# A linear-attention and SwiGLU kernel on one core: five early F blocks for six, x sums loaded earlier, query outputs stored in halves, down casts behind the SiLU

## Chip, cores and metric

One core of a Trainium2 chip runs the whole program. The metric is device time in microseconds, the median of the runs shown. The engines are TensorE (PE: matmuls, and PEld its weight loads), VectorE (DVE), ScalarE (ACT), GpSimd (POOL) and SyncE (SP, which only issues DMAs here). ACT and POOL issue some DMAs too, on queues of their own.

## What is computed

x has 2048 rows of 576 (D). With xn the row-wise layer norm of x:

```python
qkv = xn @ wqkv                                   # 32 heads of 18
phi = concat(softmax(q @ w_phi), softmax(-q @ w_phi))   # per head, for q and for k
o   = phi_q (phi_k^T v) / (phi_q (phi_k^T 1) + 1e-6)
s   = o @ wo
g   = silu((silu(xn @ w_gate) * (xn @ w_up)) @ w_down)  # F = 4608
out = x + s * g
```

All products are made from fp32r pieces: an operand is split into a high part (a cast on ACT) and a low part (a subtraction on DVE), and three products of the parts are summed.

## The kernel before, in words

**Layout.** The rows are two halves i of 1024, each of two column groups j of 512 (BT). xn is kept transposed in eight tiles X{i}{j}, `XB[i][j]` in the code (L69), 128 x 5 x 512: of D = 576, each holds two chunks of 128 rows with their low parts and a chunk of shared rows. F is 36 blocks (NF) of 128.

**Attention.** First the norm and the transposes; then, for 16 row tiles, keys and values with their softmax and the sums kv and z (L348); meanwhile GpSimd builds sums of blocks of x, stored in `sum_dram` (`sum_parts`, L316). Then the query stage (L402 to L500): for each pair of row tiles `q_tile` makes phi_q and its denominator, `numer` (L452) transposes it and multiplies by kv, and `project` (L470) multiplies by wo. `project` copies each 288-column half of its PSUM tile into the tile `so` (one buffer, 128 x 576) on ACT, and SyncE stores both halves with one DMA to `s_dram` (L483, L485).

**The feed-forward part, two forms.** A block f of F is handled either *early* or in the main stage.

- `early_tile(f, i, parts)` (L110) is the plain form: for each j, 14 matmuls of 512 columns for gate (`xw`, L82), SiLU on ACT, 14 for up, the product on DVE, and a store to `h_dram` (L121, SyncE). It needs the blocks `XB[i]`; its PSUM pool has two buffers. The first EARLY = 6 blocks go this way. They stand late in the program, so in the order that the planner writes out they fill PE's gaps in the attention stages.
- `gate_up` (L591) is the seven-product form over gate/up and the column groups (Strassen-Winograd): seven `product` calls (L566) of seven matmuls each, on sums of weights and sums of x. `gate_up_weights` (L532) loads a block's weights into `ld`, GpSimd forms the sums (L557 to L560), ACT and DVE split them (L548), and in the first pass they are stored to `w_dram` for the second. The x operands come from `operands(i)` (L511): X00, X01 and X03 stay where they are, and four sums are loaded from `sum_dram` into X10 to X13, in the place of the half i = 1 of x. So these loads wait until everything that reads `XB[1]` is done.

**Order of the early blocks.** Inside the attention part (L502): block 0 for i = 1, block 1 for i = 1 and 0, block 0 for i = 0, then blocks 2 to 4, each i = 1 first. After the attention pools are closed: block 5 for i = 1, two loads of `w_down` rows, `operands(0)`, block 5 for i = 0, the first `gate_up_weights` (L858 to L865).

**Main stage.** For i = 0 and then i = 1, 36 units (L828): the blocks from EARLY on in order, with an early block put in as every fourth unit at first (`stored`, L583, only reads `h_dram` back). The products with w_down for groups of four blocks are again a seven-product form (`strassen`, L730). They stand in a queue, and `fill()` (L846) takes items from it between the products of a unit: four calls in a gate_up unit, two in a stored one, up to two items each (three near the end). For the first group of the first pass, the casts and subtractions that prepare the items (`prep`, L799) are put behind `anchor`: `issue_after` orders instructions only on the engine of the instruction that it names, and the anchor is the last DVE product of the unit before (L630).

**What sets the order.** The program's text gives priorities; a planner turns it into a fixed order for each engine and DMA queue before the run. An instruction that waits holds those behind it on its queue. Each DMA of SyncE and ACT takes one of eight semaphores in turn, and waits for the one before it on that semaphore.

Of the kernel before, what the change touches and what calls it, by code (L numbers as in the profile page):

```python
# [9 lines left out]
F32 = mybir.dt.float32  # L10
F32R = mybir.dt.float32r
AF = mybir.ActivationFunctionType
# [4 lines left out]
S, D, H, DH, F = 2048, 576, 32, 18, 4608  # L17
P = 128
NT = S // P
BT = 512  # L20
# [3 lines left out]
HALF = D // 2  # L24
# [2 lines left out]
GROUPS = [(g * GW, min(GW, D - g * GW)) for g in range((D + GW - 1) // GW)]  # L27
NG = len(GROUPS)
QS = 256
EARLY = 6  # L30
TAILS = (NF - EARLY + 3) // 4
LAG = 3
RUSH = NF - 5
# [13 lines left out]
def gated_hedgehog_kernel(ctx: ExitStack, tc, x, w_qk, w_v, w_phi, wo, w_gu, w_tail, w_down, ident_in, mask_in, out):  # L47
# [5 lines left out]
    nc = tc.nc  # L53
# [12 lines left out]
    xpool = ctx.enter_context(tc.tile_pool(name="xpool", bufs=1))  # L66
    dram = ctx.enter_context(tc.tile_pool(name="dram", bufs=1, space=bass.MemoryType.DRAM))

    XB = [[xpool.tile([P, 5, BT], F32R, name=f"X{i}{j}") for j in range(4)] for i in range(2)]  # L69
    s_dram = dram.tile([S, D], F32, name="s_dram")  # L70
    h_dram = dram.tile([2, EARLY, P, HS], F32, name="h_dram")
    x_dram = dram.tile([2, 4, P, 4, P], F32, name="x_dram")
    sum_dram = dram.tile([2, P, 4, 4, 5, P], F32, name="sum_dram")
    w_dram = dram.tile([NF - EARLY, P, 7, 4, P], F32, name="w_dram")
    t_dram = dram.tile([TAILS, 4, 3, 32, 7, P], F32, name="t_dram")
    a_dram = dram.tile([3, P, 5, BT], F32, name="a_dram")
# [21 lines left out]
    def early_weights(f):  # L98
        parts = []
        for m in (0, 2):  # L100
            raw = epool.tile([P, 2, 3, P], F32, name="raw", bufs=2)
            hi = epool.tile([P, 2, 3, P], F32R, name="wh", bufs=3)
            lo = epool.tile([P, 2, 2, P], F32R, name="wl", bufs=3)
            nc.sync.dma_start(raw, w_gu[f, :, m:m + 2])
            with tc.high_priority():
                split_rows(hi, lo, raw)
            parts.append((hi, lo))
        return parts

    def early_tile(f, i, parts):  # L110
        for j in range(2):
            pg = eps.tile([P, BT], F32, name="pe")
            xw(pg, i, j, slice(0, BT), *parts[0], False)
            h = epool.tile([P, BT], F32, name="h")
            with tc.high_priority():
                nc.scalar.activation(h, pg, AF.Silu)
            pu = eps.tile([P, BT], F32, name="pe")
            xw(pu, i, j, slice(0, BT), *parts[1], False)
            with tc.high_priority():
                nc.vector.tensor_mul(h, pu, h)  # L120
            nc.sync.dma_start(h_dram[i, f, :, j * BT:(j + 1) * BT], h)  # L121

    with ExitStack() as att:
        const = att.enter_context(tc.tile_pool(name="const", bufs=1))
# [7 lines left out]
        with ExitStack() as kst:  # L132
# [4 lines left out]
            with ExitStack() as pst:  # L137
# [104 lines left out]
                for n in range(6):  # L242
                    k, c = divmod(n, 3)
# [104 lines left out]
            for n in range(NT):  # L348
# [8 lines left out]
                v = vbuf[n % 2]  # L357
# [44 lines left out]
        with ExitStack() as qst:  # L402
            qw = qst.enter_context(tc.tile_pool(name="qw", bufs=1))
            qk = qst.enter_context(tc.tile_pool(name="qk", bufs=2))
# [64 lines left out]

            def project(b, oh, ol):  # L470
                for j in range(QS // P):
                    so = qk.tile([P, D], F32, name="so", bufs=1)
                    jc = slice(j * P, (j + 1) * P)
                    for i in range(2):
                        n = slice(i * HALF, (i + 1) * HALF)
                        ps = qps.tile([P, 512], F32, name="p")
                        k = 0
                        for g, (o, w) in enumerate(GROUPS):
                            for a, bw in ((oh, WOH), (oh, WOL), (ol, WOH)):
                                nc.tensor.matmul(ps[:, 0:HALF], a[0:w, g, jc], bw[0:w, g, n], start=k == 0,  # L480
                                                 stop=k == 3 * NG - 1)
                                k += 1
                        nc.scalar.copy(so[:, n], ps[:, 0:HALF])  # L483
                    r0 = b * QS + j * P
                    nc.sync.dma_start(s_dram[r0:r0 + P, :], so)  # L485

            order = list(range(S // QS // 2, S // QS)) + list(range(S // QS // 2))
            es, om = None, None
# [10 lines left out]
                with tc.issue_after(last_e[3 * n // 2 + 2].ins):  # L499
                    tails(n)  # L500

        for f, halves in [(0, (1,)), (1, (1, 0)), (0, (0,))] + [(f, (1, 0)) for f in range(2, EARLY - 1)]:  # L502
            parts = first_weights.pop(0) if first_weights else early_weights(f)
            for i in halves:
                early_tile(f, i, parts)

    fw = ctx.enter_context(tc.tile_pool(name="fw", bufs=1))
    fp = ctx.enter_context(tc.tile_pool(name="fp", bufs=1, reuse_waits="tile"))
    acc = fp.tile([P, 4, HT // 2, HALF], F32, name="acc")

    def operands(i):  # L511

        xo = [None] * 7
        for n in (0, 6, 1, 3, 5, 2, 4):
            if n < 3:
                j = (0, 1, 3)[n]
                if i:
                    t = xpool.tile([P, 5, BT], F32R, name=f"X0{j}")
                    nc.sync.dma_start(t.bitcast(F32), a_dram[n])
                else:  # L520
                    t = XB[0][j]
                xo[n] = [t[:, c] for c in range(5)]
                continue
            j = n - 3
            t = xpool.tile([P, 5, BT], F32R, name=f"X1{j}")
            nc.sync.dma_start(t.bitcast(F32).rearrange("p c n -> p (c n)"),
                              sum_dram[i, :, j].rearrange("p s c n -> p (s c n)"))
            v = t.rearrange("p c n -> p (c n)").rearrange("p (s c n) -> p s c n", s=4, c=5)
            xo[n] = [v[:, :, c] for c in range(5)]
        return xo  # L530

    def gate_up_weights(i, f):  # L532

        parts, wt = {}, fw.tile([96, 7, P], F32R, name="wt", bufs=2)
        n, q = divmod(f - EARLY, 4)
        if i == 0:
# [35 lines left out]
    def short(name, bufs):  # L572
        return fq.tile([P, BT], F32, name=name, bufs=bufs)
# [17 lines left out]
    def gate_up(w, xo, fill, opening):  # L591
        A11, A12, A22, S2, S4, S3, S1 = xo
        xp, yp, wp = (fps.tile([P, BT], F32, name=n, bufs=b) for n, b in (("px", 2), ("py", 1), ("pw", 1)))
        h = h_tile()

        def snap(ps):
            t = short("s", 3)
            with tc.high_priority():
                nc.scalar.copy(t, ps)  # L599
            return t  # L600

        def add(ps, t):
            with tc.high_priority():
                nc.vector.tensor_add(t, ps, t)  # L604


        if opening:
            nc.tensor.matmul(yp, w[0][0][:, 0], A11[0], start=True, stop=True)
        product(xp, w, 0, A11, True, False)
        with tc.high_priority():  # L610
            nc.scalar.copy(yp, xp)
        product(wp, w, 4, S1, True, False)
        fill()
        product(yp, w, 1, A12, False, True)
        nc.scalar.activation(yp, yp, AF.Silu)
        product(xp, w, 5, S2, False, False)
        s2 = snap(xp)
        fill()
        product(xp, w, 2, S3, False, False)
        s3 = snap(xp)  # L620
        add(wp, s3)
        fill()
        product(xp, w, 6, A22, False, True)
        with tc.high_priority():
            nc.scalar.activation(xp, xp, AF.Silu)
        nc.vector.tensor_mul(h[1], xp, s3)  # L626
        product(wp, w, 3, S4, False, True)
        add(wp, s2)
        with tc.high_priority():
            anchor.append(nc.vector.tensor_mul(h[0], yp, s2))  # L630
        fill()
        return h
# [97 lines left out]
    def strassen(i, pairs, part, first):  # L730
# [65 lines left out]
        for f in ((p1, p7), (p4, p5, p6, p2, p3))[part]:  # L796
            hs, ws = [], []

            def prep(f=f, hs=hs, ws=ws):  # L799
                w2 = fq.tile([P, 2, 2, HALF], F32R, name="dw", bufs=3)  # L800
                with tc.issue_after(anchor[-1].ins) if first and i == 0 else ExitStack():
                    for n, g in enumerate(pairs):
                        h, w = f(g)
                        hs.append(split_h(h))
                        split(w2[:, n, 0], w2[:, n, 1], w)
                        ws.append(w2[:, n])

            n = len(pairs)
            queue.append([n, prep, [(n, lambda f=f, hs=hs, ws=ws, u=u: item(f, hs, ws, u)) for u in range(2)]])
# [19 lines left out]
    for i in range(2):  # L829
        order = [NF - 1] * i + list(range(EARLY, NF - i))  # L830
        for f in range(EARLY):
            order.insert(4 * f + 1 - i, f)
        units += [(i, n, f) for n, f in enumerate(order)]
    queue, anchor, share = [], [], [2]

    def look():
        n = 0
# [17 lines left out]

    todo = [(i, f) for i, n, f in units if f >= EARLY and (i == 0 or f < NF - 1)]
    kept = []
    parts = early_weights(EARLY - 1)  # L858
    early_tile(EARLY - 1, 1, parts)
    first_rows = [acc[:, 1].rearrange("p (a b) n -> p a (b n)", a=2)[:, n] for n in range(2)]  # L860
    for t, f in zip(first_rows, (EARLY, 0)):
        nc.sync.dma_start(t, w_down[f * P:(f + 1) * P, :])
    xo = operands(0)
    early_tile(EARLY - 1, 0, parts)
    ready = [gate_up_weights(*todo.pop(0))]  # L865
    est.close()
    fq = ctx.enter_context(tc.tile_pool(name="fq", bufs=1, reuse_waits="tile"))
# [2 lines left out]
    for i, n, f in units:  # L870
        share[0] = 2 if n < RUSH else 3
        if i == 1 and n == 0:
            xo = operands(1)
# [67 lines left out]
```

## Time and profile before

| | |
|---|---|
| median of 3 runs (lowest, highest) | 1647.22 us (1646.2, 1649.27) |
| the profiled execution's own time | 1648.95 us |
| its span, first to last instruction | 1647.0 us |
| mean granted TensorE clock | 0.998 |
| DMA moved | 264.68 MB, mean 161 GB/s |
| query stage's last projection matmul, end | 494 us |
| first feed-forward product | 540 us |

In the lines of the profile, L and a number is a line of the kernel; `out<-in` are tiles by name without buffer numbers. A group's line has its count, busy time, the mean of one in ns, and the idle time of the engine just before it with what ended that. Several instructions of PE overlap, so the mean of one is more than the distance from one to the next.

### The profile page before, as it was taken

The page shows a single profiled execution, that of the slowest core. Times are in us where ns is not written, and L with a number is a line of the kernel's source. Part 1 is how long each engine was busy: PE and PEld are TensorE (multiplying, and loading weights), DVE is VectorE, ACT ScalarE, POOL GpSimd, SP SyncE. Part 2 cuts the span into 40 slices and gives each one's busy share as a digit, 9 for nine tenths or more (in the row PEclk, how much of TensorE's full clock was granted, in tenths as well). Part 3 has the DMA queues.
Part 4 walks back from the last instruction along what each step waited for, and adds up shares of the span by engine and source line. Part 5 has one row for each costly group of instructions (what it writes and reads, how often), then busy time and mean ns, then how long its engine had stood idle before and what let it go on. Part 6 is the DMA issues. An engine that isn't in the chain of part 4 may idle for free.

```text
span 1647.0 us, 25211 instructions
## 1 busy us (share of the span) xinstructions
PE 1613.3 (98%) x9441; PEld 1436.0 (87%) x9441; DVE 1178.3 (72%) x1722; ACT 715.3 (43%) x1389; POOL 618.7 (38%) x660
## 2 busy tenths in 40 slices
PE   6999999999999999999999999999999999999998
PEld 5899998999987688888888888888888888888887
DVE  7677758989852476887887778844666677566578
ACT  5533345443431365444544445445433333333334
POOL 3467500343202344554554453422333244133132
PEclk9999999999999999999999999999999999999999
DMA  9623303343218545455455454495545556455435
GB/s 285 215 79 103 116 34 105 92 142 117 74 45 289 204 159 191 161 175 181 171 176 176 173 179 164 132 361 170 164 127 161 174 167 216 152 183 187 141 114 172
DMA packets 118107, 264.68 MB, mean 161 GB/s; under 512 B 12418, under 2 KB 48386, under 8 KB 116194
## 3 DMA queue, kind: packets, MB, share of 16 engines
q1 hardware_dynamic: 107628, 247.44, 45.0%
q0 software_dynamic: 3072, 11.02, 2.4%
q10 hardware_dynamic: 7286, 4.63, 0.9%
q8 instruction: 74, 1.21, 0.3%
q14 instruction: 47, 0.39, 0.1%
HBM read 164.21 MB, written 98.83 MB: 160 GB/s over the span
## 4 chain that ended last, share of the span: by engine, by line
PE 66%; DVE 2%; issue 1%; DMA 0%; POOL 0%; ACT 0%; SPq 0%; DVEq 0%; POOLq 0%
PE pd L669 24%; PE px L570 23%; PE pw L570 11%; PE py L570 6%; PE pe L92 2%; DVE acc L641 0%; DVE hh L59 0%; DMA hb<-h_dram 0%; DMA X<-s_dram 0%; DVE dw L59 0%; DVE w L59 0%; DVE ha L630 0%; DVE acc L642 0%; DVE s L604 0%; DVE acc L824 0%
## 5 line engine op out<-in xcount | busy, mean ns | idle before, releaser
L669 PEld LDWEIGHTS pd<-dw,hh 128*128 128x128 f32 x3048 | 431.9, 189 | 28.4 <-DVE dw L59 5.4
L669 PE MATMUL pd<-dw,hh 128*128 128x288 f32 x3048 | 448.3, 297 | 5.7 <-DVE dw L59 4.0
L570 PE MATMUL px<-X,w 128*128 128x512 f32 x1440 | 373.5, 393 | 1.5 <-ACT w L58 1.0
L570 PEld LDWEIGHTS px<-X,w 128*128 128x128 f32 x1440 | 261.3, 188 | 52.7 <-ACT s L599 3.5
L570 PE MATMUL pw<-X,w 128*128 128x512 f32 x720 | 185.5, 393 | 0.0
L570 PEld LDWEIGHTS pw<-X,w 128*128 128x128 f32 x720 | 134.7, 188 | 30.3 <-DVE s L604 0.3
L604 DVE TENSOR_TENSOR s<-pw,s 128x512 f32<-128x512 f32 x120 | 82.5, 687 | 102.6 <-ACT s L599 91.8
L92 PE MATMUL pe<-X,wh 128*128 128x512 f32 (+1 forms) x480 | 152.1, 400 | 1.7 <-POOL X L199 0.7
L794 DVE TENSOR_TENSOR acc<-pd,acc 128x576 f32<-128x576 f32 x128 | 96.1, 751 | 77.9 <-PE pd L669 77.8
L599 ACT COPY s<-px 128x512 f32<-128x512 f32 x120 | 70.3, 586 | 155.1 <-PE px L570 154.9
L59 DVE TENSOR_TENSOR hh<-ha,hh 128x512 fp32r<-128x512 f32 x140 | 115.5, 850 | 14.8 <-ACT hh L58 13.8
L58 ACT CAST hh<-ha 128x512 fp32r<-128x512 f32 x140 | 82.7, 619 | 95.4 <-PE pd L669 72.2
L92 PE MATMUL p<-KVWH,X 128*128 128x288 f32 (+1 forms) x640 | 123.6, 298 | 0.4 <-DVE phi L274 0.4
L766 POOL TENSOR_TENSOR hb<-hb 128x512 f32<-128x512 f32 x34 | 46.4, 1364 | 164.1 <-DVE hb L626 163.6
L92 PEld LDWEIGHTS pe<-X,wh 128*128 128x128 f32 (+1 forms) x480 | 88.5, 189 | 19.7 <-DVE h L120 1.5
L92 PEld LDWEIGHTS p<-KVWH,X 128*128 128x128 f32 (+1 forms) x640 | 100.5, 188 | 1.1 <-issue 0.8
L59 DVE TENSOR_TENSOR w<-ld,w 128x512 fp32r<-128x512 f32 (+1 forms) x90 | 76.2, 847 | 31.9 <-ACT w L58 30.5
L570 PE MATMUL px<-X,wt 96*128 96x512 f32 x240 | 94.8, 395 | 0.0
L570 PE MATMUL py<-X,w 128*128 128x512 f32 x360 | 94.0, 394 | 0.1
L779 POOL TENSOR_TENSOR ha<-ha 128x512 f32<-128x512 f32 x34 | 52.4, 1556 | 109.5 <-DVE hh L59 109.5
L58 ACT CAST w<-ld 128x512 fp32r<-128x512 f32 (+1 forms) x90 | 49.4, 549 | 87.5 <-POOL ld L560 55.2
L753 POOL TENSOR_TENSOR h<-ha,hb 128x512 f32<-128x512 f32 x34 | 45.4, 1334 | 100.7 <-DVE ha L630 66.6
(181 smaller groups left out, 3044.1 us busy)
## 6 DMA issues: line engine op xcount, KB each, us to landing
w_dram<-w SPq DMA_DIRECT2D x87, 512.0 KB, 2.8
w<-w_dram SPq DMA_DIRECT2D x87, 512.0 KB, 4.4
wt<-t_dram SPq DMA_DIRECT2D x59, 336.0 KB, 3.5
ld<-in_B_w_gu SPq DMA_DIRECT2D x30, 512.0 KB, 4.5
X<-sum_dram SPq DMA_DIRECT2D x8, 1280.0 KB, 6.8
rt<-in_B_w_down SPq DMA_DIRECT2D x33, 288.0 KB, 3.9
rb<-in_B_w_down SPq DMA_DIRECT2D x33, 288.0 KB, 4.0
w_dram<-w SPq DMA_DIRECT2D x29, 256.0 KB
```

Of the source, the lines that this page charges most:

```text
L58: nc.scalar.copy(hi, src)
L59: nc.vector.tensor_sub(lo, src, hi)
L92: nc.tensor.matmul(ps, l, r, start=n == 0, stop=n == len(pairs) - 1)
L570: nc.tensor.matmul(ps, l, r, start=first and n == 0, stop=last and n == len(mm) - 1, skip_group_check=True)
L599: nc.scalar.copy(t, ps)
L604: nc.vector.tensor_add(t, ps, t)
L669: nc.tensor.matmul(ps, l, r, start=first and n == 0 and m == 0, stop=n == len(hs) - 1 and m == 2, skip_group_check=True)
L753: sub(s, g["h"][0][0], g["h"][0][1])
L766: nc.gpsimd.tensor_add(a21, a21, g["h"][1][1])
L779: sub(a12, a12, g["h"][0][0])
L794: nc.vector.tensor_add(a2, pd[:, :, 0:HALF], a2)
```

## The change

EARLY goes from 6 to 5. `operands` moves ahead of the attention part, and `operands(0)` is called inside it, behind the last early tile of half i = 1. Block 0 for i = 0 moves to the end of the early tiles. Each half of a query output gets a tile of its own (two buffers of 128 x 288), stored by ACT right behind its copy. The SiLU of the xp product is remembered in `last_act`, and the preparation of the first group's down products is also ordered behind it, on ACT. TAILS stays 8.

```diff
-EARLY = 6
+EARLY = 5
...
-                    so = qk.tile([P, D], F32, name="so", bufs=1)
                     jc = slice(j * P, (j + 1) * P)
+                    r0 = b * QS + j * P
                     for i in range(2):
...
-                        nc.scalar.copy(so[:, n], ps[:, 0:HALF])
-                    r0 = b * QS + j * P
-                    nc.sync.dma_start(s_dram[r0:r0 + P, :], so)
+                        so = qk.tile([P, HALF], F32, name="so", bufs=2)
+                        nc.scalar.copy(so, ps[:, 0:HALF])
+                        nc.scalar.dma_start(s_dram[r0:r0 + P, n], so)
...
-        for f, halves in [(0, (1,)), (1, (1, 0)), (0, (0,))] + [(f, (1, 0)) for f in range(2, EARLY - 1)]:
+        for f, halves in [(0, (1,))] + [(f, (1, 0)) for f in range(1, EARLY)] + [(0, (0,))]:
             parts = first_weights.pop(0) if first_weights else early_weights(f)
             for i in halves:
                 early_tile(f, i, parts)
+                if (f, i) == (EARLY - 1, 1):
+                    xo = operands(0)
...
         with tc.high_priority():
-            nc.scalar.activation(xp, xp, AF.Silu)
+            last_act.append(nc.scalar.activation(xp, xp, AF.Silu))
...
-                with tc.issue_after(anchor[-1].ins) if first and i == 0 else ExitStack():
+                with ExitStack() as order:
+                    if first and i == 0:
+                        order.enter_context(tc.issue_after(anchor[-1].ins))
+                        order.enter_context(tc.issue_after(last_act[-1].ins))
                     for n, g in enumerate(pairs):
...
-    parts = early_weights(EARLY - 1)
-    early_tile(EARLY - 1, 1, parts)
     first_rows = [acc[:, 1].rearrange("p (a b) n -> p a (b n)", a=2)[:, n] for n in range(2)]
     for t, f in zip(first_rows, (EARLY, 0)):
         nc.sync.dma_start(t, w_down[f * P:(f + 1) * P, :])
-    xo = operands(0)
-    early_tile(EARLY - 1, 0, parts)
     ready = [gate_up_weights(*todo.pop(0))]
```

More of the change, by code (lines that the diff above doesn't have):

```diff
@@ L121, in early_tile, with operands @@
             nc.sync.dma_start(h_dram[i, f, :, j * BT:(j + 1) * BT], h)
+    def operands(i):
+        xo = [None] * 7
+        for n in (0, 6, 1, 3, 5, 2, 4):
+            if n < 3:
+                j = (0, 1, 3)[n]
+                if i:
+                    t = xpool.tile([P, 5, BT], F32R, name=f"X0{j}")
+                    nc.sync.dma_start(t.bitcast(F32), a_dram[n])
+                else:
+                    t = XB[0][j]
+                xo[n] = [t[:, c] for c in range(5)]
+                continue
+            j = n - 3
+            t = xpool.tile([P, 5, BT], F32R, name=f"X1{j}")
+            nc.sync.dma_start(t.bitcast(F32).rearrange("p c n -> p (c n)"),
+                              sum_dram[i, :, j].rearrange("p s c n -> p (s c n)"))
+            v = t.rearrange("p c n -> p (c n)").rearrange("p (s c n) -> p s c n", s=4, c=5)
+            xo[n] = [v[:, :, c] for c in range(5)]
+        return xo
     with ExitStack() as att:
@@ L509, in gated_hedgehog_kernel @@
     acc = fp.tile([P, 4, HT // 2, HALF], F32, name="acc")
[L511 to L530, printed above, removed]
     def gate_up_weights(i, f):
@@ L833, in gated_hedgehog_kernel @@
         units += [(i, n, f) for n, f in enumerate(order)]
-    queue, anchor, share = [], [], [2]
+    queue, anchor, last_act, share = [], [], [], [2]
     def look():
```

## Prediction

> **What bounds the kernel now.** First the share of each engine and the engines on the chain that ended last:
>
> ```profile
> PE 1613.3 (98%) x9441; PEld 1436.0 (87%) x9441; DVE 1178.3 (72%) x1722; ACT 715.3 (43%) x1389; POOL 618.7 (38%) x660
> ...
> PE 66%; DVE 2%; issue 1%; DMA 0%; POOL 0%; ACT 0%; SPq 0%; DVEq 0%; POOLq 0%
> ```
>
> TensorE (PE) is busy for 1613.3 of 1647.0 us. The other 33.7 us is all that any reordering could win; a larger gain has to take matmuls away. Next I read the windows by stage, to see whether some stretch is bound by another engine.
>
> ```profile
> 300.00:400.00 100.00, 98.79 (x689) 91.74 (x688) 89.16 (x136) 47.41 (x85) 41.95 (x84) 1.00 0.43 130
> 400.00:500.00 100.00, 99.95 (x649) 89.72 (x648) 73.28 (x116) 39.05 (x72) 14.86 (x30) 1.00 0.24 76
> 800.00:1000.00 200.00, 200.00 (x1094) 176.22 (x1093) 154.59 (x225) 96.99 (x194) 97.58 (x95) 1.00 0.50 175
> ```
>
> The columns are PE, PE's weight loads, DVE, ACT, POOL, granted clock, DMA share and GB/s. In the query stage (the first two rows) PE is full although DVE is at 89% in one of them: the chain softmax, numerator, projection leaves gaps, and early tiles stand in them. In the feed-forward stage (the third row) PE is full with DVE at 77%. So a matmul removed in either stage shortens the kernel by its pitch, if nothing opens a gap. Where PE does stand, the waits view says:
>
> ```profile
> PE tp L189 <- DVE xn L177: 11.6, 2, 10.5
> PE pd L669 <- DVE dw L59: 4.0, 3, 1.5
> ...
> PE p L480 <- ACT so L483: 1.2, 2, 0.6
> PE px L570 <- ACT w L58: 1.0, 2, 0.5
> ```
>
> (total us, times, longest). The last three are in the code that the change edits. The longest, 11.6 us for the first transposes, is at the start, which the change leaves alone.
>
> **Term 1: a block moves from the plain form to the seven-product form.** An early tile is 56 matmuls of 512 columns: two row halves j, gate and up, 14 each. The trace counts them:
>
> ```profile
> L92 PE MATMUL pe<-X,wh 128*128 128x512 f32 x384 | 139.9, 400 | 1.0 <-DVE h L120 0.6 <-DVE X L192 0.4
> L92 PE MATMUL pe<-X,wl 128*128 128x512 f32 x192 | 76.6, 399 | 0.0
> L92 PE MATMUL pe<-X,wh 96*128 96x512 f32 x96 | 38.3, 399 | 0.7 <-POOL X L199 0.7
> ```
>
> 384 + 192 + 96 = 672, or 112 for each of six blocks (two row halves i). The same block in gate_up is seven products of seven matmuls, 49 for each i, so 98. The change removes 14 matmuls. The mean of 400 ns is not what one costs, since they overlap; the pitch is read from unbroken stretches of the chain that ended last:
>
> ```profile
> 504.10 36.27 PE pe L92 x154
> ...
> 580.72 1.61 PE pd L669 x12
> 582.33 1.63 PE px L570 x7
> ```
>
> 36.27 / 154 = 0.2355 us for an early matmul, 1.63 / 7 = 0.2329 us for one of a product. So 112 x 0.2355 = 26.4 us goes and 98 x 0.2329 = 22.8 us comes: **-3.6 us**. [...]
>
> What comes with the block: two more gate_up units, each with two snaps, a copy and two SiLU on ACT, two adds and two products on DVE, and in the first pass its weight casts on both. Priced from these rows,
>
> ```profile
> L604 DVE TENSOR_TENSOR s<-pw,s 128x512 f32<-128x512 f32 x120 | 82.5, 687 | 102.6 <-ACT s L599 91.8
> L59 DVE TENSOR_TENSOR w<-ld,w 128x512 fp32r<-128x512 f32 x60 | 52.3, 872 | 14.0 <-ACT w L58 13.7
> ```
>
> DVE gets 4 x 0.69 + 4 x 0.87 = about 6.2 us beside 49 matmuls of 11.4 us. The place is unit 21 of 36, past the middle of each pass; the window above, from the first pass, shows that DVE has a quarter free, so I cost it at nothing (with DVE full it would be the 6.2 us of one unit, less what PE does meanwhile); its neighbours are already gate_up units back to back. The extra loads and stores (one block of w_dram, one h_dram block less) stand beside a DMA share of 0.50.
>
> **Term 2: the query outputs in halves.** Today one full so tile is filled by two copies and stored by SyncE; the next copy waits for the landing:
>
> ```profile
> ACT so L483 <- DMA s_dram<-so: 10.1, 4, 2.7
> ...
> L483 ACT COPY so<-p x32: 381/399/406, 300.3 to 493.8; 128x288 f32<-128x288 f32 x32
> ...
> 464.16 6.12 SPq L485 DMA_DIRECT2D s_dram<-so  x2
> ...
> s_dram<-so SPq DMA_DIRECT2D x16, 288.0 KB, 2.9
> ```
>
> ACT stood 10.1 us for it and passed 1.2 us on to PE (p L480 above). After the change a half buffer is used again two groups later: 30 matmuls of 288 columns at 1.61 / 12 = 0.134 us are 4.0 us, against a copy of 0.40, an issue and a landing of at most 2.9. It just fits, so I take the whole **-1.2 us** (bounds 0 and -1.2). What it adds is 32 issues on ACT's own queue. The nearest rows:
>
> ```profile
> L200 ACTq DMA_DIRECT2D x_dram<-xr x8: 365/389/822, 19.9 to 73.0; - x8
> L699 ACTq DMA_DIRECT2D y_dram<-acc x8: 520/520/596, 1088.6 to 1120.9; - x8
> ```
>
> 32 x 0.39 to 0.52 = 12.5 to 16.6 us of ACT in 190 us where it is 39 to 47% busy, and 10.1 us of waiting goes. Behind each issue on ACT stand the casts of ph and oh and the SiLU of the early tiles, for which PE waits next; the rows of PE show no wait on those today. I take 0, with +1.5 as the upper bound (the ratio of the so wait, 1.2 of PE for 10.1 of ACT, on 12.5 us). SyncE loses 16 stores and their waits, so h stores, weight loads and the x sums get past sooner. [...]
>
> **Term 3: less cover at the opening.** The sixth early block was what PE did while the first feed-forward weights were made. What is left to do when the last projection has ended (494 us):
>
> ```profile
> 494.00:540.40 46.40, 46.05 (x196) 36.50 (x195) 4.81 (x7) 4.18 (x7) 1.00 0.79 278
> ...
> 493.77 0.57 SPq L539 DMA_DIRECT2D ld<-in_B_w_gu  x1
> ...
> 502.43 1.01 DVE L59 TENSOR_TENSOR w<-ld,w 128x512 fp32r<-128x512 f32 x2
> ```
>
> The first row is of the tile pe alone: 196 early matmuls follow the query stage. If that stage takes in as many as before, 196 - 112 = 84 remain, 84 x 0.2355 = 19.8 us. The first weights need from the issue at 493.8 to 503.4, 9.7 us. So 10 us of cover is left over and the edit costs **0**. The x sums:
>
> ```profile
> 519.13 0.32 SPq L526 DMA_DIRECT2D X<-sum_dram  x1
> ...
> 528.50 0.88 SPq L526 DMA_DIRECT2D X<-sum_dram  x2
> ...
> ld<-in_B_w_gu SPq DMA_DIRECT2D x30, 512.0 KB, 4.5
> X<-sum_dram SPq DMA_DIRECT2D x8, 1280.0 KB, 6.8
> ```
>
> They are issued as the last tile of half i = 1 frees the blocks. In the new order that tile is the third from the end instead of the second, so 112 matmuls (26.4 us) follow it, against 56 (13.2 us) now; four landings of 6.8 us, even one after the other (27.2 us), are nearly inside, and the first product needs none of them. Zero again.
>
> **Term 4: the first down casts behind the SiLU.** On ACT today, around 600 us:
>
> ```profile
> 598.78 0.62 ACT L58 CAST hh<-ha 128x512 fp32r<-128x512 f32 x1
> 599.30 0.43 ACT L58 CAST dw<-acc 128x288 fp32r<-128x288 f32 x1
> 599.63 0.43 ACT L58 CAST dw<-rb 128x288 fp32r<-128x288 f32 x1
> 599.96 0.58 ACT L625 ACTIVATE px<-px 128x512 f32<-128x512 f32 x1
> 601.07 0.62 ACT L58 CAST w<-ld 128x512 fp32r<-128x512 f32 x1 [0.53 <-PE pw L570]
> ```
>
> Three casts run right ahead of the SiLU and can hold it by their 1.2 us at most (starts 598.78 to 599.96). Turned round, they would partly fill the idle 0.53 behind it. But what PE waits for is the other engine:
>
> ```profile
> 603.95 1.53 DVE L59 TENSOR_TENSOR dw<-td,dw 128x288 fp32r<-128x288 f32 x1
> ...
> 608.20 1.33 PE L669 MATMUL pd<-dw,hh 128*128 128x288 f32 x8 [1.54 <-DVE dw L59]
> ```
>
> DVE's subtractions are already held behind the last product of the unit, and one took 1.53 us. Moving ACT's half does not move them. I take **0**; the bounds are -5.0 (all of pd <- dw, 4.0, and px <- ACT w, 1.0, go) and +3.0 (two more waits of 1.5 us, when the casts come so late that DVE stands for ACT).
>
> **Sum.** -3.6 - 1.2 = -4.8 us. The profiled execution took 1648.95 us by its own time, 1.95 more than its span; the median of the runs shown is 1647.22, or 1.73 below it. From the median the sum gives **1642.4 us**, -0.29%. The forecast's own range is 1639.9 (half of term 4's lower bound) to 1645.1 (term 2 at 0 and ACT's issues at +1.5).
>
> **Rivals.** (a) The opening's waits go too: terms 1 and 2 and another -5.0 at most, 1637.4. For it: 5.0 us of PE waits stand exactly where ACT's order changes. Against: DVE's 1.53 us.
> (b) The order is planned anew and loses elsewhere what term 2 wins: +3.0 as in term 4, 1645.4, within 0.2%. For it: the opening has to run with less than half of its former cover (19.8 of 46 us).
> (c) Slower: ACT stands behind the x sums. Its stores take the same eight DMA semaphores in turn as SyncE's transfers; this row shows it at such a semaphore before seven of eight stores:
>
> ```profile
> L699 ACTq EVENT_SEMAPHORE x7: 17/17/17, 1087.9 to 1120.0; - x7
> ```
>
> There it cost 17 ns each. But in the new order four loads of 1280 KB (5.24 MB) fall into the query stage; at the 278 GB/s of the row at 494 us they take 18.9 us together, and a store whose turn comes after one of them waits on ACT that long. PE can run two early PSUM tiles (28 matmuls, 6.6 us) without ACT; beyond that it stops. Price 18.9 - 6.6 = 12.3 us: 1654.7. It decides from a stand of 6.6 us on. Against: eight transfers usually span more than that.
> (d) The change does not do what it says: the x sums delay the first weights instead. If the first ld waits behind all four (18.9 us instead of its landing of 4.5), 14.4 us are added to 9.7, or 24.1 against a cover of 19.8: 1646.7, no gain that shows.
>
> **Chances.** About 0.2% (3.3 us) is what a measurement of this kernel can tell from no change; faster means under 1643.9. Forecast 0.46, (a) 0.14, (b) 0.20, (c) and its like 0.14, (d) 0.06. Faster is the forecast and (a), 0.60; within 0.2% is (b) and (d), 0.26; slower is (c), 0.14. The range reaches from (a) to the middle of no change, 1637.4 to 1648.0, and leaves out (c) and a little on each side.
>
> **What would show it.** 9427 matmuls instead of 9441; 560 early ones and 98 more in L570. No PE wait for so. A solid stretch of some 84 early matmuls before the first product, not 196, and that product near 513 us. X loads before 500 us. Wrong I would be if PE shows a wait of over 2 us between 470 and 520, or if ACT stands for a DMA semaphore there (c), or if pd <- dw falls well below 4.0 (a).

## The result, and the profile after

The changed kernel takes **1651.43 us** (median of 10 runs, 1650.8 to 1655.5) against 1648.72 us (10 runs, 1646.2 to 1650.36) for the kernel before on the same chip: a ratio of **1.0023, 95% interval 1.0014 to 1.0031**. It is slower by 0.23%, or 3.8 us by the ratio, where 1642.4 was forecast. Below, us are worked out from ratios times 1648.7; an interval of a ratio is about 0.09% or 1.5 us to each side.

The profiled execution took 1652.48 us by its own time, with a span of 1650.3. Engines, and the engines of the chain that ended last, by the page of the changed kernel:

```profile
PE 1611.3 (98%) x9427; PEld 1433.7 (87%) x9427; DVE 1175.3 (71%) x1726; ACT 724.9 (44%) x1401; POOL 625.9 (38%) x664
...
PE 63%; DVE 2%; issue 0%; DMA 0%; ACT 0%; DVEq 0%; SPq 0%; ACTq 0%
```

The 14 matmuls are gone (9427 for 9441) and PE is busy for 2.0 us less, yet the span is 3.3 us longer. So PE stands more, or runs slower, somewhere. What PE waits for in the changed kernel (total us, times, longest; its L572, L613 and L671 are L570, L611 and L669 of before):

```profile
PE py L572 <- ACT py L613: 5.8, 5, 2.3
PE pd L671 <- DVE dw L59: 3.7, 3, 2.0
...
PE px L572 <- ACT w L58: 0.8, 2, 0.5
```

The first row is new: 5.8 us in five waits for a copy on ACT that is not among the rows of before. The wait for so is gone, as forecast. The stretches show where it happens. The 30 us from the first feed-forward product on, and the 60 us behind them, first in the changed kernel:

```profile
512.70:542.70 30.00, 25.05 (x95) 18.15 (x94) 10.91 (x14) 9.01 (x17) 16.73 (x19) 0.94 0.79 266
542.70:602.70 60.00, 53.52 (x285) 45.47 (x284) 41.80 (x55) 34.15 (x69) 29.75 (x28) 1.00 0.47 159
```

and in the kernel before:

```profile
540.20:570.20 30.00, 28.39 (x118) 21.45 (x117) 13.04 (x17) 11.78 (x24) 12.05 (x14) 1.00 0.65 224
570.20:630.20 60.00, 55.94 (x303) 47.91 (x303) 44.77 (x59) 35.32 (x70) 33.88 (x32) 1.00 0.46 162
```

Columns: PE, its weight loads, DVE, ACT, POOL, granted clock, DMA share, GB/s. PE is idle for 30.00 - 25.05 = 4.95 us instead of 1.61, and then for 6.48 instead of 4.06: 5.8 us more in the 90 us. The clock of 0.94 in the first row is one stretch of 3.413 us at half speed (from 534.38 us on), by estimate another 1.7 us (half of it). Together 7.5 us are lost, against the 4.8 us that the removed matmuls and the wait for so were to bring. That leaves +2.7 of the +3.3 us by which the spans differ; the rest is spread too thinly to be put anywhere.

**The first chain, 3 us behind the first product.** From the timeline of the changed kernel: the queue of SyncE, then ACT, then PE.

```profile
498.37 0.57 SPq L541 DMA_DIRECT2D ld<-in_B_w_gu  x1
...
505.20 2.87 SPq L552 DMA_DIRECT2D w_dram<-w  x2
...
509.69 0.88 SPq L552 DMA_DIRECT2D w_dram<-w  x2
510.62 0.97 SPq L541 DMA_DIRECT2D ld<-in_B_w_gu  x1
...
516.26 0.62 ACT L58 CAST w<-ld 128x512 fp32r<-128x512 f32 x1 [7.14 <-DMA ld<-in_B_w_gu]
516.79 0.58 ACT L613 COPY py<-px 128x512 f32<-128x512 f32 x1
...
517.42 0.96 PE L572 MATMUL py<-X,w 128*128 128x512 f32 x3 [1.12 <-ACT py L613]
```

The load `ld` of the first block is issued at 498.4; that of the second stands on SyncE behind the four stores of the first block's split weights, which wait for those to be made. It goes out at 510.6. ACT idles for 7.14 us until it lands, and the copy that PE needs stands behind the cast of it. The copy's own input had been there since 514.7 us.

**The second chain, 18 us behind the first product**, in the same view:

```profile
523.53 0.45 SPq L729 DMA_DIRECT2D rb<-in_B_w_down  x1
...
529.01 1.21 POOL L756 TENSOR_TENSOR td<-rb,rt 128x288 f32<-128x288 f32 x1 [3.78 <-DMA rb<-in_B_w_down]
...
531.93 0.72 POOL L562 TENSOR_TENSOR ld<-ld,ts 128x256 f32<-128x256 f32 x1
...
532.69 0.41 ACT L58 CAST w<-ld 128x256 fp32r<-128x256 f32 x1 [4.03 <-POOL ld L562]
533.00 0.58 ACT L613 COPY py<-px 128x512 f32<-128x512 f32 x1
...
533.63 2.32 PE L572 MATMUL py<-X,w 128*128 128x512 f32 x6 [2.28 <-ACT py L613]
```

Here a row of w_down lands late; GpSimd stands for it with the last piece of the third block's weights behind it, ACT stands for that piece with the copy behind it, and PE for the copy.

**The third chain, 82 us behind the first product**, is where the SiLU order works:

```profile
578.70 0.58 ACT L627 ACTIVATE px<-px 128x512 f32<-128x512 f32 x1 [0.96 <-PE px L572]
579.19 0.61 ACT L58 CAST hh<-ha 128x512 fp32r<-128x512 f32 x1
...
581.55 0.62 ACT L58 CAST w<-ld 128x512 fp32r<-128x512 f32 x1
...
586.49 1.33 PE L671 MATMUL pd<-dw,hh 128*128 128x288 f32 x8 [1.98 <-DVE dw L59]
...
590.61 0.68 DVE L59 TENSOR_TENSOR w<-ld,w 128x512 fp32r<-128x512 f32 x1
...
592.39 0.94 POOL L562 TENSOR_TENSOR ld<-ld,ts 128x256 f32<-128x256 f32 x1
...
593.68 0.58 ACT L613 COPY py<-px 128x512 f32<-128x512 f32 x1
...
594.31 1.66 PE L572 MATMUL py<-X,w 128*128 128x512 f32 x6 [1.66 <-ACT py L613]
```

Behind the SiLU of 578.70 now stand six casts for the down products (579.19 to 581.22), and the weight cast of 581.55 comes after them. DVE's half of that split (590.61) has come to stand behind eight subtractions for the down products. GpSimd overwrites `ld` with the next weight piece only when that half has read it, and in its order the piece (592.39) now stands behind seven sums for the down products. In the kernel before the same piece came before those sums, right behind DVE's half, 62 us behind the first product instead of 80:

```profile
601.07 0.62 ACT L58 CAST w<-ld 128x512 fp32r<-128x512 f32 x1 [0.53 <-PE pw L570]
...
601.92 0.68 DVE L59 TENSOR_TENSOR w<-ld,w 128x512 fp32r<-128x512 f32 x1
...
602.74 0.74 POOL L560 TENSOR_TENSOR ld<-ld,ts 128x256 f32<-128x256 f32 x1 [5.84 <-DVE w L59]
```

So the planner, given one more order on ACT, put the same work on DVE and GpSimd in another order too. In all five profiles with the SiLU order, here and below, this piece stands behind the seven sums; in the eight without it, it comes ahead of them.

### The profile page after: what moved, and what is told of

It reads as the page before. It is cut to its first block, busy times and chain, and to the rows that moved or that the text cites. A ratio compares the mean times of both kernels' runs of the same rounds, so it can differ in the third digit from the quotient of the medians.

```text
span 1650.3 us, 25223 instructions
## 1 busy us (share of the span) xinstructions
PE 1611.3 (98%) x9427; PEld 1433.7 (87%) x9427; DVE 1175.3 (71%) x1726; ACT 724.9 (44%) x1401; POOL 625.9 (38%) x664
## 4 chain that ended last, share of the span: by engine, by line
PE 63%; DVE 2%; issue 0%; DMA 0%; ACT 0%; DVEq 0%; SPq 0%; ACTq 0%
PE pd L671 23%; PE px L572 23%; PE pw L572 11%; PE py L572 6%; DVE acc L643 0%; DVE hh L59 0%; DVE dw L59 0%; DMA X<-s_dram 0%; DVE s L606 0%; DVE acc L644 0%; DVE ha L632 0%; DVE w L59 0%; DVE acc L829 0%; ACT py L613 0%; DVE X L796 0%
## 5 line engine op out<-in xcount | busy, mean ns | idle before, releaser
L671 PEld LDWEIGHTS pd<-dw,hh 128*128 128x128 f32 x3048 | 432.5, 188 | 28.3 <-DVE dw L59 4.6
L671 PE MATMUL pd<-dw,hh 128*128 128x288 f32 x3048 | 449.0, 297 | 5.4 <-DVE dw L59 3.7
L572 PE MATMUL px<-X,w 128*128 128x512 f32 x1488 | 386.6, 394 | 1.9 <-ACT s L601 0.9
L572 PEld LDWEIGHTS px<-X,w 128*128 128x128 f32 x1488 | 270.9, 189 | 55.6 <-ACT s L601 4.8
L572 PE MATMUL pw<-X,w 128*128 128x512 f32 x744 | 191.8, 393 | 0.0
L572 PEld LDWEIGHTS pw<-X,w 128*128 128x128 f32 x744 | 139.2, 188 | 31.1
L92 PE MATMUL pe<-X,wh 128*128 128x512 f32 (+1 forms) x400 | 128.0, 400 | 2.1 <-DVE h L120 1.1
L59 DVE TENSOR_TENSOR hh<-ha,hh 128x512 fp32r<-128x512 f32 x140 | 110.7, 816 | 17.2 <-ACT hh L58 16.0
L572 PE MATMUL py<-X,w 128*128 128x512 f32 x372 | 97.9, 397 | 5.8 <-ACT py L613 5.8
L572 PE MATMUL px<-X,wt 96*128 96x512 f32 x248 | 97.9, 395 | 0.0
L92 PEld LDWEIGHTS pe<-X,wh 128*128 128x128 f32 (+1 forms) x400 | 73.7, 189 | 16.9 <-DVE h L120 2.0
```

Source lines behind the costliest of these rows:

```text
L59: nc.vector.tensor_sub(lo, src, hi)
L92: nc.tensor.matmul(ps, l, r, start=n == 0, stop=n == len(pairs) - 1)
L572: nc.tensor.matmul(ps, l, r, start=first and n == 0, stop=last and n == len(mm) - 1, skip_group_check=True)
L671: nc.tensor.matmul(ps, l, r, start=first and n == 0 and m == 0, stop=n == len(hs) - 1 and m == 2, skip_group_check=True)
```

## The experiments

Two theories stood at first. **Cover**: with one block less of early matmuls, loads that were hidden end in PE's way. **Casts**: the order behind the SiLU delays the casts, and so PE. Each predicts which single part costs. The medians of the kernel before beside which these were run are 1649.31, 1648.76 and 1648.45 us (35, 32 and 21 runs).

### One part at a time

The changed kernel without the SiLU order:

```diff
-                with ExitStack() as order:
-                    if first and i == 0:
-                        order.enter_context(tc.issue_after(anchor[-1].ins))
-                        order.enter_context(tc.issue_after(last_act[-1].ins))
+                with tc.issue_after(anchor[-1].ins) if first and i == 0 else ExitStack():
```

> The changed kernel without the ordering of the down casts behind the SiLU. Theory of the cover (the opening waits because the sixth block no longer covers the second block's weights): the two early waits of PE for the py copy (1.1 and 2.3 us) stay, and the time stays near 1651.4. Theory of the casts (the down casts behind the SiLU push the next block's weight cast back): the two later waits for the py copy (0.6 near 568 us and 1.7 near 594 us) go, about -2.3, near 1649.1. Both may hold; then the early waits stay and the late ones go.

Measured: 1647.75 us, ratio 0.9997 (0.9987 to 1.0006). The two late waits for py (0.58 and 1.66 us) are gone; the two early ones are 0.66 and 1.42 us for 1.12 and 2.28.

The changed kernel with six early blocks:

```diff
-EARLY = 5
+EARLY = 6
```

> The changed kernel with EARLY = 6 and all else as changed. Theory of the cover: the early part of the opening's new waits goes (0.8 + 1.1 + 2.3, and the 1.7 us lost to the half clock after it, about 5.9 in all) and 3.6 us of matmuls come back: near 1649.1. If the cover does not matter: 1651.4 + 3.6 = 1655.0. Theory of the casts: the waits near the first down products stay.

Measured: 1649.15 us, ratio 1.0007 (0.9999 to 1.0016).

The kernel before with the halves of the query output alone:

```diff
-                    so = qk.tile([P, D], F32, name="so", bufs=1)
...
-                        nc.scalar.copy(so[:, n], ps[:, 0:HALF])
-                    nc.sync.dma_start(s_dram[r0:r0 + P, :], so)
+                        so = qk.tile([P, HALF], F32, name="so", bufs=2)
+                        nc.scalar.copy(so, ps[:, 0:HALF])
+                        nc.scalar.dma_start(s_dram[r0:r0 + P, n], so)
```

> The kernel before with the query outputs in halves on ACT alone. The prediction's term 2: -1.2, 1647.5 against 1648.7, and no PE wait for so. If ACT's 32 issues cost PE what the buffer gives: 1648.7 to 1650.

Measured: 1648.21 us, ratio 0.9995 (0.9987 to 1.0004).

The kernel before with the SiLU order alone:

```diff
-            nc.scalar.activation(xp, xp, AF.Silu)
+            last_act.append(nc.scalar.activation(xp, xp, AF.Silu))
...
+                        order.enter_context(tc.issue_after(last_act[-1].ins))
```

> The kernel before with the down casts ordered behind the SiLU alone. The prediction's term 4: 0, 1648.7. Theory of the casts: new waits of PE for the py copy behind the first down products, about +2.3, near 1651. Theory of the cover alone: no change.

Measured: 1651.68 us, ratio 1.0013 (1.0005 to 1.0022).

What follows. The SiLU order costs wherever it stands: 1.0013 alone (+2.1 us, the interval leaves out zero), 1.0007 against 0.9995 with six blocks and halves (+2.0; the first of these also has the x sums and block 0 in their new places, which no run tried alone), 1.0023 against 0.9997 in the change (+4.3). So the casts theory holds. But without that order the change is still at 0.9997 where two gains should show, so something else eats about as much. The cover theory would explain it, and the next runs test that. The halves gain 0.8 us, with an interval that takes in zero.

The profiles show where the SiLU order costs. Below, a py product is the matmuls into py that stand behind the copy on ACT. In the changed kernel that of the third chain starts 25.6 us behind the one before it (568.71 to 594.31). The same distance is 25.6 us in all five profiles with the SiLU order, with five early blocks and with six, and 24.0 to 24.2 us in the eight without it: 1.5 us. One py product earlier the distance is 19.6 us with the order and 18.9 without (where no stretch at half clock lies in it): 0.7 us. With six blocks no wait of 1.66 us for py is seen, because PE is at half clock from 605.7 to 609.1 us (granted 0.50) and is busy instead, for 3.40 of 3.40 us; but the py product comes as late, 7.82 us behind the end of the wait for dw, as it does in the changed kernel (586.49 to 594.31). From the timeline of the changed kernel with six blocks:

```profile
605.60 2.22 PE L671 MATMUL pd<-dw,hh 128*128 128x288 f32 x8 [1.98 <-DVE dw L59]
...
613.42 1.66 PE L572 MATMUL py<-X,w 128*128 128x512 f32 x6
```

### The loads behind the stores

The first two chains above were attacked one by one, in the changed kernel without the SiLU order. First the place of the second block's weight load: the first block's stores to w_dram, which only the second pass reads, are held until that load is issued.

```diff
-                if f < NF - 1:
+                if f == EARLY:
+                    held.append((w_dram[f - EARLY, :, m:m + k], w))
+                elif f < NF - 1:
                     nc.sync.dma_start(w_dram[f - EARLY, :, m:m + k], w.bitcast(F32))
...
+        while held and f > EARLY:
+            dst, w = held.pop(0)
+            nc.sync.dma_start(dst, w.bitcast(F32))
```

> The changed kernel without the SiLU order (1647.75), and the first block's 14 stores to w_dram stand on SyncE behind the second block's weight loads. Theory (less cover costs, and it does so because the second block's ld is issued behind these stores, 510.6 us in the changed kernel): ld is issued some 4 to 5 us earlier, the two TensorE waits 3 to 12 us behind the first product (0.8 and 1.05 us) go, and the time falls by 1 to 2 us to about 1646.2. Rival (the wait is of the casts' own place on ScalarE, not of the load): the waits stay, 1647.7. Rival (the stores moved back only move the wait to the next loads in line, rt and rb): the waits at 3 to 12 us go and the one near 18 us grows by as much, 1647.7.

(The stores held are four, not 14.) Measured: **1644.16 us, ratio 0.9975 (0.9964 to 0.9986)**, the best of all. Of this kernel the issue of the second load on SyncE:

```profile
501.10 0.56 SPq L543 DMA_DIRECT2D ld<-in_B_w_gu  x1
```

the first 30 us of products:

```profile
511.60:541.60 30.00, 27.51 (x114) 20.63 (x114) 11.85 (x17) 11.46 (x22) 12.82 (x16) 1.00 0.84 290
```

and the wait for py, 2.1 us in two without this edit:

```profile
PE py L579 <- ACT py L620: 0.7, 1, 0.7
```

The load goes out 10.5 us ahead of the first product, where it was 2.1 us in the same kernel without this edit (508.1 for a first product at 510.2). PE is idle for 2.49 us in these 30 us, against 4.95 in the changed kernel. Without the SiLU order but with the late load it was 4.20 us:

```profile
510.20:540.20 30.00, 25.80 (x106) 19.12 (x105) 10.54 (x14) 11.77 (x23) 17.35 (x19) 1.00 0.83 284
```

The step from 0.9997 to 0.9975 is 3.6 us, about twice the idle time that went here (1.7) and over twice what was expected; the 60 us behind gain another 0.5. The remaining 1.4 us lie within the intervals. The rival that the stores only move the wait to rt and rb fell: the wait near 18 us shrank too, from 1.4 us to 0.7.

Second, the down rows of the second pair of blocks loaded ahead of the main stage:

```diff
-                    g["top"] = down_rows(g["f"][0], "rt")
-                    g["bottom"] = down_rows(g["f"][1], "rb")
+                    g["top"], g["bottom"] = soon.pop(0) if soon else (down_rows(g["f"][0], "rt"),
+                                                                      down_rows(g["f"][1], "rb"))
...
+    soon = [(down_rows(units[2][2], "rt"), down_rows(units[3][2], "rb"))]
```

> The changed kernel without the SiLU order (1647.75), with the w_down rows rt and rb of the second pair of blocks loaded ahead of the main stage instead of behind the stores to w_dram. Theory (the wait of 1.58 us for py 18 us behind the first product comes from rb landing late, which holds GpSimd's sum td, then its ld piece, then ScalarE's cast): the wait goes, the time falls by 1.5 us or so to about 1646.2, more if the clock fell behind that wait. Rival (GpSimd is late by its own work): the wait stays within 0.5 us, 1647.7.

Measured: 1647.92 us, ratio 1.0002 (0.9992 to 1.0012). The waits of this kernel:

```profile
PE px L572 <- ACT s L601: 3.2, 3, 1.9
...
PE py L572 <- ACT py L613: 1.0, 1, 1.0
```

The wait for py at 18 us is gone, but one of 1.9 us for a copy s took its place some 14 us behind the first product: the casts of the down products now come early and stand on ACT ahead of that copy, waiting for GpSimd. My theory of the second chain named the right wait and the wrong cure; no gain. Both edits:

> Both of these edits in the changed kernel without the SiLU order. If the two chains are what less cover costs: the waits of the first 30 us of the main stage fall from about 6.4 us lost to about 3.6, as with six blocks, and the early block saved shows: about 1645 (1647.75 less 2.8). If the loads only change places: 1647.7.

Measured: 1644.89 us, ratio 0.9980 (0.9970 to 0.9989), no better than the first edit alone. So one load's place carries most of what less cover costs.

### Do the two costs add, and is it the cover?

The changed kernel whole, SiLU order included, with the held stores:

> The changed kernel whole, SiLU order included, with the first block's four stores to w_dram (four, not the 14 written for the run before) behind the second block's weight loads. Theory (the SiLU order and the late load are two costs that add): the load's place is worth 3.6 us as without the SiLU order, 1651.43 to about 1647.8, and 3.6 us above the 1644.16 of that run. Rival (the SiLU order costs only because the load is late, both at ScalarE's casts): 1644.2.

Measured: 1646.99 us, ratio 0.9989 (0.9981 to 0.9998). The SiLU order again costs, 0.9989 against 0.9975 or 2.3 us, so it does not cost only because the load is late: with the load mended, its wait of 1.7 us in the third chain is still there. Whether the two costs add exactly, the runs do not show (4.3 us with the late load, 2.3 without).

The kernel before, six early blocks, with the held stores and nothing else:

> The kernel before with its first block's four stores to w_dram behind the second block's weight loads, nothing else. Theory (the place of the load costs only where the cover behind it is short; the kernel before has 46 us of early matmuls there): no difference, 1648.7. Rival (the gain of 3.6 us is the store's own place and has nothing to do with five blocks): about 1645.2.

Measured: 1648.25 us, ratio 0.9998 (0.9989 to 1.0007). The held stores bring nothing here, as the cover theory has it: with 46 us of early matmuls left, the late load is hidden.

One block less still, held stores, no SiLU order:

```diff
-EARLY = 5
+EARLY = 4
```

> The changed kernel without the SiLU order, the stores held as before, and EARLY 4: a second block moves to the seven-product form. If 3.6 us per block holds and the loads still come in time: 1644.16 less 3.6, 1640.6. Rival (the cover left is now shorter than what the second block's loads and sums need): 3 to 5 us of TensorE waits return in the first 30 us of the main stage, 1644 to 1646, more if the clock halves behind one.

Measured: 1657.87 us, ratio **1.0055 (1.0042 to 1.0067)**: 9 us slower. Of this kernel the timeline (PE, SyncE, ACT, PE), and the windows around its long wait:

```profile
489.76 0.29 PE L501 MATMUL p<-WOH,ol 72*128 72x288 f32 x1
...
490.08 0.57 SPq L543 DMA_DIRECT2D ld<-in_B_w_gu  x1
...
494.93 0.62 ACT L58 CAST w<-ld 128x512 fp32r<-128x512 f32 x1 [4.44 <-DMA ld<-in_B_w_gu]
...
495.60 0.79 PE L617 MATMUL py<-X,w 128*128 128x512 f32 x1 [5.55 <-ACT w L58]
```

```profile
491.00:494.40 3.40, 0.00 (x0) 0.00 (x0) 0.00 (x0) 0.00 (x0) 0.00 (x0) 1.00 0.87 279
494.40:497.80 3.40, 2.20 (x5) 1.74 (x6) 0.95 (x2) 1.41 (x3) 2.67 (x4) 0.50 1.06 340
```

Now no early matmul at all is left behind the last projection, the first weights are the bound, PE, DVE, ACT and GpSimd stand for them, and the clock is at half behind it. This could have been read from the profile of the changed kernel. Its window of the tile pe alone, behind the query stage:

```profile
498.00:512.70 14.70, 13.71 (x57) 10.54 (x57) 1.37 (x2) 1.19 (x2) 1.00 0.74 266
```

57 early matmuls, so the stages before took in 560 - 57 = 503; four blocks have 448 in all.

### The clock behind a wait

The changed kernel with 13 matmuls of 512 columns into a PSUM tile that nobody reads, 4 in the first unit and 9 in the second, ahead of the products that waited for the copy:

```diff
+        return ins
...
-        product(wp, w, 4, S1, True, False)
+        ins = product(wp, w, 4, S1, True, False)
+        if spare:
+            idle = fps.tile([P, 2, 512], F32, name="pd", bufs=2)
+            with tc.issue_after(ins.ins):
+                for _ in range(spare):
+                    nc.tensor.matmul(idle[:, 0], w[0][0][:, 0], A11[0], start=True, stop=True)
```

> The changed kernel (1651.43) with 13 more matmuls of 512 columns into a PSUM tile that nobody reads, 4 in the first and 9 in the second gate_up unit of the first pass, behind the product wp and ahead of the one that waited 1.12 and 2.28 us. It computes nothing that is used. Theory (TensorE's pause of 2.28 us itself brings the half clock of 3.413 us behind it): the wait is filled, the half-clock stretch near 534 us goes and the mean granted clock rises from 0.9966 to about 0.9976, 1649.7. Rival (the clock falls for another reason): the 13 matmuls lie in the waits or cost 3.0 us at most, the clock stays at 0.9966, 1651.4 to 1654.4.

Measured: 1649.82 us, ratio 1.0008 (0.9999 to 1.0017): with 13 matmuls more, 1.6 us less by the medians. Of the changed kernel, and then of this one, the window with the wait and the one behind it:

```profile
531.00:534.40 3.40, 1.12 (x5) 0.67 (x4) 1.03 (x1) 0.89 (x2) 3.24 (x5) 1.00 0.57 211
534.40:537.80 3.40, 3.40 (x9) 2.64 (x8) 0.69 (x1) 1.10 (x2) 1.24 (x2) 0.50 0.76 250
```

```profile
530.70:534.10 3.40, 3.40 (x17) 2.80 (x16) 0.30 (x1) 0.95 (x2) 1.29 (x1) 1.00 0.95 352
534.10:537.50 3.40, 3.40 (x16) 2.60 (x15) 1.66 (x2) 1.26 (x3) 2.62 (x3) 1.00 0.44 176
```

With PE filled, the clock stays at 1.00 here, and from 534.0 to 540.0 us PE has 24 matmuls, where it had 19 in the changed kernel at a mean clock of 0.72. There the next py product starts 15.48 us behind the one before it (533.63 to 549.11), where it is 13.77 us in the kernel before (556.96 to 570.73): 1.7 us, as much as half of 3.413. But two such stretches come later in this profile which the changed kernel's does not have:

```profile
547.80:551.20 3.40, 3.40 (x12) 3.11 (x13) 2.79 (x6) 0.62 (x1) 1.12 (x1) 0.50 0.01 3
585.40:588.80 3.40, 3.40 (x10) 2.64 (x9) 3.40 (x4) 0.64 (x1) 2.15 (x3) 0.50 0.00 0
```

What the first costs is put at 1.7 us, an estimate (half of 3.413). The second stands at the third chain, where such a stretch cost nothing with six early blocks (the py product 7.82 us behind the end of the wait for dw with it and, in the changed kernel, without). The mean granted clock over all runs rose from 0.9966 to 0.9974 (0.9979 for the kernel before, in another set of runs). The intervals of the two ratios overlap a little. So the half clock is a cost of its own in this one place; how much of the 1.6 us between the medians it is, is not settled.

## Why the prediction was wrong, step by step

**Term 1 held.** 9427 matmuls, 560 early ones. With the load mended and no SiLU order, five blocks against six with halves is 0.9975 against 0.9995: -0.20%, or -3.3 us, where -3.6 was worked out (the place of the x sums differs too).

**Term 2 held in its wait**, its size is not settled: the wait for so is gone, and -0.8 us was measured (-2.1 to +0.7) for -1.2. The 32 issues cost ACT less than the rows used:

```profile
L506 ACTq DMA_DIRECT2D s_dram<-so x32: 326/326/344, 300.5 to 498.8; - x32
```

32 x 0.326 = 10.4 us, and in the changed kernel PE shows no wait between 300 and 500 us.

**Term 3 failed, at the words "So 10 us of cover is left over and the edit costs 0".** The count was for the first block's weights alone, and for these it was right: PE does not wait at the first product. But cover is used up by everything that comes late in a row. The second block's load stands on SyncE behind four stores that wait for the first block's casts; the kernel before has the same order there, and hid it. Measured: 3.6 us without the SiLU order. The number of 84 early matmuls was off too. There were 57, since the query stage took in 27 more; its end moved from 494 to 498 us, and the first product came at 512.7, so the 513 was right by luck, from two errors that cancel. The x sums were indeed free: they were issued from 433.8 to 470.8 us.

**Term 4 failed, at "Moving ACT's half does not move them".** It was taken as 0, with bounds of -5.0 and +3.0. It cost 2.0 to 2.3 us in three comparisons and 4.3 in the change. Two things moved that the step left where they were. First the other half of each split: DVE's subtractions wait for ACT's casts, and the two waits of pd for dw that were 0.92 and 1.54 us became 0.23 and 1.98; together they are no longer than they were. Second, and this is the cost, the weight casts: they now stand behind the down casts, the planner put their subtraction and GpSimd's next weight piece behind the down products' work as well, and the py product that waits for this comes 1.5 us later, the one before it 0.7 us. That is 2.2 us in the profiles, as in the three comparisons. The upper bound (DVE stands for ACT) had the first of these; that an order on one engine makes the planner lay out two others anew stood in rival (b), and term 4's own working left it out.

**The sum**: -0.8 (halves) - 3.3 (block) + 3.6 (late load) + 2.1 (SiLU order) = +1.6 us, against a measured +3.8. The first three terms make the 0.9997 without the SiLU order by how they were taken, so the sum tests only the last. The missing 2.2 is the SiLU order in the presence of the late load, 4.3 and not 2.1. An estimate from the intervals of the ratios leaves about 2.5 us to each side of that difference, so the runs do not show that the two costs are more than their sum. The profiles offer one cause: behind the wait of 2.28 us the changed kernel has a stretch at half clock, 15.48 us to the next py product for 13.77 in the kernel before, and without the SiLU order the wait there is 1.42 us and no such stretch follows. Between after and before the mean granted clocks, 0.9966 and 0.9979, differ by 0.0013 x 1650 = 2.1 us. That fits, but the two are of different sets of runs, and no run separates the clock from the rest.

**Rivals.** (b) came nearest in kind: both a new order and less cover. But its +3.0 was one price for what came twice, and the clock beside it. (a), (c) and (d) fell: px <- ACT w is 0.8 for 1.0, the semaphore waits of ACT's stores are 17 ns each, the first ld was not held up. The sign I had set, a PE wait of over 2 us between 470 and 520, looked in the wrong place: the wait of 2.28 us ended at 533.6, with the third block.

## What to carry to other kernels

When work that covers a start is taken away, count the cover against every transfer that is in order behind the first, not the first alone, and look on the issuing queue for stores that wait for something: a store that nobody needs soon does not belong ahead of a load. An order put on one engine is an order for all that follow from it: read what the moved instructions now stand ahead of, on every engine of the chain, not only who was last in the waits view. If an edit brings a gain and a loss, run its parts alone: here leaving out one part brought 1.0023 to 0.9997, and moving one load to 0.9975.

## What the runs showed of the hardware

The half-clock stretches lie on a grid of 3.4133 us. In the kernel before they begin at 18.70 and 1643.45 us, 476 x 3.4133 us apart, in the changed kernel at 534.38 and 1647.13 us, 326 x 3.4133 apart. The two of the filler's kernel (547.80 and 585.40 us) and the two of the SiLU order on the kernel before (572.60 and 610.10) are 37.6 and 37.5 us apart, where 11 x 3.4133 is 37.55. Those of the kernel before and of the changed kernel last 3.413 us but for the end of the span (5.7 and 5.6); with four early blocks one lasts about twice that (a mean clock of 0.51 from 494.4 to 501.3 us). The SiLU order on the kernel before has a wait of 1.98 us (606.99 to 608.97) that falls within one window:

```profile
606.70:610.10 3.40, 1.42 (x11) 1.18 (x10) 3.40 (x4) 1.25 (x4) 3.24 (x4) 1.00 0.02 5
610.10:613.50 3.40, 3.40 (x10) 2.66 (x9) 3.40 (x4) 0.64 (x1) 2.14 (x3) 0.51 0.00 0
```

In the changed kernel the same wait of 1.98 us (584.51 to 586.49) is cut by the grid at 585.58, and no half clock follows:

```profile
582.20:585.60 3.40, 2.09 (x14) 1.62 (x12) 3.40 (x4) 2.85 (x6) 3.32 (x3) 1.00 0.42 109
585.60:589.00 3.40, 2.51 (x14) 2.29 (x15) 3.40 (x5) 0.64 (x1) 2.62 (x4) 1.00 0.00 0
```

Four timelines have this wait of 1.98 us: in two of them (the SiLU order on the kernel before, the changed kernel with six blocks, 603.62 to 605.60) it lies within one window and half speed follows, from 610.1 and from 605.7 us. In the other two (the changed kernel, and the same with the held stores, 577.45 to 579.43, where a window of 3.4 us begins at 578.0) it is cut and none follows.

In the 3.4 us ahead of a half-speed stretch PE was busy for 0.00 us (four early blocks), 1.12 (the changed kernel), 1.19 (the same with six blocks), 1.42 and 1.70 (the SiLU order on the kernel before) and 1.84 (the kernel before with held stores). Of the grid's windows behind which the clock stayed at 1.00, from the first product to 1640 us, the lowest have 1.75 and 1.85 us in the changed kernel and 1.86 and 1.89 in the kernel before. So of these windows each with 1.42 us or less was followed by half speed, and between 1.70 and 1.89 it went both ways; PE's busy time as the profile models it isn't the whole measure. In the changed kernel a half-speed stretch went with 1.7 us more to the next py product (15.48 us for 13.77 in the kernel before); behind the wait of 1.98 us it took nothing with six blocks (7.82 us from the wait's end to the py product with it and, in the changed kernel, without).
